# Attention and mixture of experts on one core: a planner's order against a written software pipeline of 25 iterations

## The chip, the core and the metric

The kernel runs on one core of a Trainium2 chip. A core has four engines that compute: TensorE (PE; its weight loads are listed apart as PEld), VectorE (DVE), ScalarE (ACT) and GpSimd (POOL). SyncE (SP) issues most of the transfers here; sixteen DMA engines carry them out. Each engine works through its own queue in order, and waits on semaphores for the others. The metric is the device time of one execution in microseconds (us).

## What is computed

An attention over 8 batches of 8 heads, with 576 positions of 64 elements, gives 4608 rows of 512; a mixture of 8 experts then works on these rows. Cut to what matters:

```python
def _attn_ref(q, k, v):
    q_d, k_d, v_d = mean over each 4 positions       # 144 pooled positions
    out_up = np.repeat(sm_attn(q_d, k_d, v_d), 4, axis=2)
    mask = np.abs(pos[:, None] - pos[None, :]) < 4   # a band of 7 positions
    scores = np.where(mask, scale * q @ k.T, -1e9)
    out_local = softmax(scores) @ v
    return out_up + out_local

def _moe_ref(x, ...):
    logits = x @ w_gate + modality_bias[modality_id]
    e_idx = np.argmax(logits, axis=1)
    for e in range(8):
        h = np.maximum(x[e_idx == e] @ w1[e], 0.0)
        out[e_idx == e] = gate_w[...] * (h @ w2[e])
```

All inputs and outputs are float32.

## The kernel before

The attention runs over 32 steps, one for each pair of heads (b, hp): 8 batches of 4 pairs. Step n of the loop in `build` (L764) holds pieces of several pairs at once.

- `load_qk` (L188) loads q and k of two pairs in eight transfers of [96 partitions, 6 rows of 64]; `load_v` (L199) loads a batch's v in 23 windows of up to 32 positions into `vw`, one buffer for even and one for odd batches; `load_vg` (L213) loads v of one pair for the pooling. All are issued from SP.
- `pre` (L225) transposes q and k on TensorE (L238) into PSUM tiles of tag T, which has three buffers, copies them out on ACT (q, L243) and DVE (k, L245), and adds up groups of four (DVE L248, POOL L252 and L253). `pool_v` (L217) does the same for v on POOL.
- `scores` (L259), one step later: the band scores as 46 small matmuls (L275) on a mask, whose maxima and differences DVE takes (L278, L279), the exponential (L280), and the pooled scores (L286) with their maximum (DVE L290) and exponentials (ACT L294).
- `softmax` (L297), two steps later: sums and reciprocals (DVE L301 to L304), products on POOL (L306, L317), a 32x32 transpose on DVE (L309) and four copies on ACT that lay the weights out as a band in the buffer `Pw` (L312). Three buffers `Pw` take turns.
- `av` (L316), three steps later (LAG): transposes of the pooled weights (PE L327, ACT L330), products with v (L334, evicted as `Od` by ACT at L337; L344), and their sum into the tile X (DVE L352). The second batch of a pair starts 64 columns into its tile, so that the last 64 positions of the first go into X of the next.
- The router works once a batch: `logits` (L386, L388), `choose` (16 small DVE instructions and an exponential, L399 to L422), `place` (PE L429 to L433, DVE L436 to L440), `scatter` (four or five indirect transfers from POOL into a table, L445) and `rows` (PE L459, ACT L460 and a transfer from SP, L462), which writes the rows back for the experts.

The order in which an engine's queue holds these pieces is set by a planner, which takes the program's order as priority, puts instructions where its own model of time says that they are ready, and adds the semaphores. Some pieces have a higher priority (`hip`). A constant table adds six matmuls on a zero tile at step 4 (BZ, L777). In the steps from 25 on, two first groups of rows are gathered for the experts ("early", L837 to L848), and their matmuls start while the attention still runs. After the attention come 18 groups of 256 rows and one of 128, each with the weights of one expert, split into a high and a low part.

Of the kernel before, what the change touches and what calls it, by code (L numbers as in the profile page):

```python
# [42 lines left out]
N0,N1,N2 = (2,3,4)  # L43
PV = 0
AN = 2
LEAD = 8
ST = 1
NPW = 3
# [4 lines left out]
HIP = 1  # L53
GO = 1
LS = 1
VD = 0
NCE = (2,1,1)
BZ = (0,0,0,0,6)
# [104 lines left out]
class Attention:  # L163
    def __init__(s, tc, ctx, ectx, C, psum, q, k, v):
        s.tc, s.C, s.ps = tc, C, psum
        nc = s.nc = tc.nc
        s.q, s.k, s.v = q, k, v

        s.ld = ectx.enter_context(tc.tile_pool(name="ald", bufs=2, side="right", reuse_waits="tile"))
        s.wk = ctx.enter_context(tc.tile_pool(name="awk", bufs=2, reuse_waits="tile"))  # L170
        s.one = ctx.enter_context(tc.tile_pool(name="aone", bufs=1, reuse_waits="tile"))
        s.QK, s.V, s.VG = {}, {}, {}
# [3 lines left out]
        s.clear(0)  # L176

    def clear(s, j):

        nc = s.nc  # L180
        if j < 2:
            nc.vector.memset(s.kT[j][:, 0:PAD], 0.0)
            nc.vector.memset(s.kT[j][:, S + PAD :], 0.0)
            nc.vector.memset(s.vw[j][0:32, 0], 0.0)
            nc.vector.memset(s.vw[j][64:96, NB - 1], 0.0)
        (nc.vector if j == 0 else nc.gpsimd).memset(s.Pw[j], 0.0)

    def load_qk(s, b, half):  # L188
        nc = s.nc

        qt = s.ld.tile([96, 2, 6, 2, D], F32, name="qt")
        kt = s.ld.tile([96, 2, 6, 2, D], F32, name="kt")
        for g in range(2):
            for t, src in ((qt, s.q), (kt, s.k)):
                for a in range(2):
                    nc.sync.dma_start(t[:, g, :, a], src[b, 4 * half + 2 * g + a].rearrange("(j p) d -> p j d", j=6))
        s.QK[b, half] = (qt, kt)

    def load_v(s, b):  # L199
        nc = s.nc  # L200
        vd = s.wk.tile([72, H, 2, D], F32, name="vd")
        vw = s.vw[b % 2]
        s.V[b] = (vw, vd)

        for i in range(NB):
            for j in range(4):
                lo = BLK * i + SUB * j - PAD
                k0, k1 = max(lo, 0), min(lo + WIN, S)
                if lo + PAD < S:
                    nc.sync.dma_start(vw[32 * j + k0 - lo : 32 * j + k1 - lo, i],  # L210
                                      s.v[b, :, k0:k1].rearrange("h p d -> p h d"))

    def load_vg(s, b, hp):  # L213
        vg = s.VG[b, hp] = s.ld.tile([72, 2, 512], F32, name="vg", bufs=2)
        s.nc.sync.dma_start(vg, s.v[b, 2 * hp : 2 * hp + 2].rearrange("h (p t) d -> p h (t d)", t=8))

    def pool_v(s, b, hp):  # L217
        nc = s.nc
        v5 = s.VG.pop((b, hp)).rearrange("p h (c t d) -> p (h c) t d", c=2, t=4)
        t1 = s.ld.tile([72, 4, 2, D], F32, name="vt", bufs=2)  # L220
        nc.gpsimd.tensor_tensor(t1, v5[:, :, 0:2], v5[:, :, 2:4], op=ALU.add)
        (nc.vector if VD else nc.gpsimd).tensor_tensor(
            s.V[b][1][:, 2 * hp : 2 * hp + 2].rearrange("p h c d -> p (h c) d"), t1[:, :, 0], t1[:, :, 1], op=ALU.add)

    def pre(s, b, hp):  # L225
        nc, C = s.nc, s.C
        outs = []
        for nm, src in zip("qk", s.QK[b, hp // 2]):
            if nm == "q":
                Tm = T = s.ld.tile([128, S], F32, name="qT")  # L230
            else:
                T = s.kT[hp % 2]
                Tm = T[:, PAD : PAD + S]
            for i in range(2):

                p = s.ps.tile([128, 3, 96], F32, name="tp", tag="T", bufs=3)
                for j in range(3):
                    nc.tensor.transpose(p[:, j, :], src[:, hp % 2, 3 * i + j].rearrange("p a d -> p (a d)"),  # L238
                                        C.ident[:96, :96])
                x = Tm[:, 288 * i : 288 * i + 288]  # L240
                p = p.rearrange("m j p -> m (j p)")
                if nm == "q":
                    nc.scalar.mul(x, p, QS)  # L243
                else:
                    nc.vector.tensor_copy(x, p)  # L245
            dd = s.wk.tile([128, 144], F32, name=nm + "d")
            if nm == "q":
                nc.vector.tensor_reduce(dd, Tm.rearrange("m (g t) -> m g t", t=4), op=ALU.add, axis=AX.X)  # L248
            else:
                d2 = s.ld.tile([128, 144, 2], F32, name="d2", bufs=1)  # L250
                T4 = Tm.rearrange("m (g t) -> m g t", t=4)
                nc.gpsimd.tensor_tensor(d2, T4[:, :, 0:2], T4[:, :, 2:4], op=ALU.add)  # L252
                nc.gpsimd.tensor_tensor(dd.rearrange("m (c g) -> m g c", c=2),  # L253
                                        d2[:, :, 0].rearrange("m (g c) -> m g c", c=2),
                                        d2[:, :, 1].rearrange("m (g c) -> m g c", c=2), op=ALU.add)
            outs += [T, dd]
        return outs

    def scores(s, b, hp, qT, qd, kT, kd):  # L259
        nc, C = s.nc, s.C  # L260
        n = 2 * NB
        m = s.wk.tile([128, n], F32, name="lm")
        e = s.wk.tile([128, n, WIN], F32, name="le", bufs=3)
        for a in range(2):
            p = s.ps.tile([128, NB, WIN], F32, name="sc", tag="S", bufs=3)
            r = slice(64 * a, 64 * a + 64)
            g = slice(NB * a, NB * a + NB)
            nc.tensor.matmul(p, C.identb, C.mask, start=True, stop=False, skip_group_check=True)
# [11 lines left out]
        nc.scalar.activation(e, e, AF.Exp, scale=0.125 / QS)  # L280
        el = e
        p = s.ps.tile([128, 3, 144], F32, name="scd", tag="S", bufs=3)
        for c in range(3):
            for a in range(2):
                r = slice(64 * a, 64 * a + 64)
                nc.tensor.matmul(p[r, c, :], qd[r, 40 * c : 40 * c + 64], kd[r, :], start=True, stop=True,  # L286
                                 skip_group_check=True)
        m = s.wk.tile([128, 3], F32, name="dm")
        e = s.wk.tile([128, 3, 144], F32, name="de", bufs=3)
        nc.vector.tensor_reduce(m, p, op=ALU.max, axis=AX.X, negate=True)  # L290

        z = s.wk.tile([128, 5, 4], F32, name="z")
        for c in range(3):
            nc.scalar.activation(e[:, c], p[:, c], AF.Exp, bias=m[:, c : c + 1], accum_out=z[:, 4, c : c + 1])  # L294
        return el, (e, z)

    def softmax(s, b, hp, e, de):  # L297
        nc = s.nc
        n = 2 * NB
        ed, z3 = de  # L300
        nc.vector.tensor_reduce(z3[:, :4, :3], e.rearrange("p (r c) w -> p r c w", c=3), op=ALU.add, axis=AX.X)  # L301
        z = s.wk.tile([128, n + 3], F32, name="zr")
        nc.vector.tensor_scalar(z, z3[:, :, :3], 1e-9, None, op0=ALU.add)
        nc.vector.reciprocal(z, z)  # L304
        Pw = s.Pw[(4 * b + hp) % NPW]
        nc.gpsimd.tensor_tensor(e, e, z[:, :n].unsqueeze(2).broadcast_to([128, n, WIN]), op=ALU.mult)  # L306

        eT = s.wk.tile([128, n, WIN], F32, name="lt")
        nc.vector.transpose(eT.rearrange("p n w -> p (n w)"), e.rearrange("p n w -> p (n w)"))  # L309
        for j in range(4):  # L310
            r = slice(32 * j, 32 * j + 32)
            nc.scalar.copy(Pw[r, :, j, :SUB], eT[r, :, :SUB])  # L312
        if 4 * b + hp < AN:
            for c in range(3):
                nc.scalar.mul(ed[:, c], ed[:, c], z[:, n + c : n + c + 1])
        else:  # L316
            nc.gpsimd.tensor_tensor(ed, ed, z[:, n:].unsqueeze(2).broadcast_to([128, 3, 144]), op=ALU.mult)  # L317
        return Pw, ed

    def av(s, b, hp, Pw, Ed, dst):  # L320
        nc, C = s.nc, s.C
        vw, vd = s.V[b]
        PdT = s.wk.tile([72, 2, 2, 144], F32, name="PdT")
        for kc in range(2):
# [5 lines left out]
            nc.scalar.copy(PdT[:, kc].rearrange("p a (c r) -> p c a r", c=3), src)  # L330
        pd = s.ps.tile([128, 144], F32, name="avd", tag="A", bufs=2)
# [4 lines left out]
        Od = s.wk.tile([128, 144], F32, name="Od")  # L336
        nc.scalar.mul(Od, pd, 0.25)  # L337
        for i0, i1 in ((0, 3), (3, NB)):
            t0, t1 = BLK * i0, min(BLK * i1, S)
# [6 lines left out]
            p = p.rearrange("m i j q -> m (i j q)")  # L346
            for x, r0, r1, off in dst:
# [4 lines left out]
                nc.vector.tensor_tensor(  # L352
# [384 lines left out]
def build(tc, q, k, v, mid, w_gate, bias, w1, w2, out):  # L737
    nc = tc.nc
    with ExitStack() as ctx:
# [8 lines left out]
        with ExitStack() as actx:  # L748
# [6 lines left out]
            at.load_qk(0, 0)  # L755
            at.load_qk(0, 1)
            C.load(tc, cp, work, ro.wk, mid, bias, w_gate)
            at.load_v(0)
            at.load_vg(0, 0)
            steps = [(b, hp) for b in range(B) for hp in range(4)]  # L760
            hip = (lambda: tc.high_priority()) if HIP else ExitStack
            N = len(steps)
            st, X = {}, {}
            for n in range(N + LAG):  # L764
                if n < N:
                    b, hp = steps[n]
                    if hp % 2 == 0 and n + 2 < N and n > 0 or n == 0:
                        b2, h2 = steps[n + 2]
                        if (b2, h2 // 2) not in at.QK:
                            at.load_qk(b2, h2 // 2)  # L770
                    if n % 4 == 3 and b + 1 < B:
                        at.load_v(b + 1)
                    st[n] = at.pre(b, hp)
                if n < NPW - 1:
                    at.clear(n + 1)
                if n < len(BZ):
                    C.busy(nc, BZ[n])  # L777
                if n == N0:
# [160 lines left out]
```

## Time and profile before

| | us |
|---|---|
| median of three runs | 808.2 |
| lowest and highest | 801.91, 811.26 |
| the profiled execution's time | 799.32 |
| its span, first to last instruction | 797.6 |

A profile was taken of one execution, with each instruction's start, duration and waits. In its lines, L12 is line 12 of the kernel; `out<-in` are tiles; a number behind x is a count. A line of a group ends with the engine's idle time ahead of these instructions and what ended it. A line of the queue of SP or of another engine's own transfers has a q (SPq, POOLq). Busy times over the span, as shares: PE 93%, DVE 59%, ACT 53%, POOL 40%. The transfers moved 150.00 MB in 205075 packets, of which 132683 are under 512 bytes: a row of 64 elements of q, k or v is 256 bytes.

### The profile page before, as it was taken

The page shows a single profiled execution, that of the slowest core. Times are in us where ns is not written, and L with a number is a line of the kernel's source. Part 1 is how long each engine was busy: PE and PEld are TensorE (multiplying, and loading weights), DVE is VectorE, ACT ScalarE, POOL GpSimd, SP SyncE. Part 2 cuts the span into 40 slices and gives each one's busy share as a digit, 9 for nine tenths or more (in the row PEclk, how much of TensorE's full clock was granted, in tenths as well). Part 3 has the DMA queues.
Part 4 walks back from the last instruction along what each step waited for, and adds up shares of the span by engine and source line. Part 5 has one row for each costly group of instructions (what it writes and reads, how often), then busy time and mean ns, then how long its engine had stood idle before and what let it go on. Part 6 is the DMA issues. An engine that isn't in the chain of part 4 may idle for free. (4 is left out here: it accounts for less than half of the span.)

```text
span 797.6 us, 20726 instructions
## 1 busy us (share of the span) xinstructions
PE 739.1 (93%) x8185; PEld 616.6 (77%) x8185; DVE 469.4 (59%) x957; ACT 426.5 (53%) x882; POOL 319.2 (40%) x362
## 2 busy tenths in 40 slices
PE   8488999899989988899799999999999999999995
PEld 5366767576767666778699888999998899999884
DVE  7534757574657667858476555556555555655520
ACT  4534657474747356855466555545555554555520
POOL 5525565665574658323353333233222333222000
PEclk9685989897989679999989999999999999999998
DMA  8769967577868597334889766677666667666500
GB/s 143 149 135 179 202 132 201 104 177 138 209 125 210 98 235 189 110 108 176 283 275 321 253 207 227 213 249 237 229 227 220 216 225 233 224 217 231 186 13 18
DMA packets 205075, 150.00 MB, mean 188 GB/s; under 512 B 132683, under 2 KB 171631, under 8 KB 204976
## 3 DMA queue, kind: packets, MB, share of 16 engines
q1 hardware_dynamic: 196720, 129.43, 59.5%
q0 software_dynamic: 8256, 19.22, 6.8%
q8 instruction: 65, 1.06, 0.6%
q14 instruction: 34, 0.28, 0.2%
HBM read 129.40 MB, written 19.47 MB: 187 GB/s over the span
## 5 line engine op out<-in xcount | busy, mean ns | idle before, releaser
L613 DVE TENSOR_TENSOR wlo<-raw,whi 128x1024 fp32r<-128x1024 f32 x130 | 160.2, 1245 | 130.4 <-ACT whi L612 120.7
L612 ACT CAST whi<-raw 128x1024 fp32r<-128x1024 f32 x130 | 134.7, 1049 | 120.2 <-PE l L677 54.3
L677 PE MATMUL l<-xh,whi 128*128 128x256 f32 x488 | 138.8, 286 | 0.7 <-ACT xh L660 0.7
L677 PE MATMUL l<-xh,wlo 128*128 128x256 f32 x488 | 138.4, 284 | 0.0
L677 PE MATMUL l<-xl,whi 128*128 128x256 f32 x488 | 138.3, 284 | 0.0
L728 POOL DMA_INDIRECT out_dram<-o,tg x37 | 40.9, 1105 | 173.3 <-ACT o L727 127.7
L724 PE MATMUL l<-wlo,hh 128*128 128x512 f32 x256 | 100.4, 393 | 0.0
L724 PE MATMUL l<-whi,hl 128*128 128x512 f32 x256 | 100.4, 393 | 0.0
L724 PE MATMUL l<-whi,hh 128*128 128x512 f32 x256 | 98.7, 397 | 0.0
L677 PEld LDWEIGHTS l<-xh,whi 128*128 128x128 f32 x488 | 93.3, 192 | 2.5 <-ACT xh L660 1.1
L677 PEld LDWEIGHTS l<-xl,whi 128*128 128x128 f32 x488 | 93.4, 191 | 0.6
L677 PEld LDWEIGHTS l<-xh,wlo 128*128 128x128 f32 x488 | 93.3, 191 | 0.2 <-issue 0.2
L275 PEld LDWEIGHTS sc<-kT,qT 64*26 64x26 f32 (+1 forms) x2944 | 40.7, 104 | 36.6 <-issue 27.3
L275 PE MATMUL sc<-kT,qT 64*26 64x32 f32 (+1 forms) x2944 | 60.7, 199 | 8.9 <-issue 8.4
L626 POOL DMA_INDIRECT tg<-tab,midx x33 | 38.1, 1154 | 75.3 <-DMA out_dram<-o,tg 69.5
L680 DVE SCALAR_TENSOR_TENSOR hl<-l,hh 128x512 fp32r<-128x512 f32 x72 | 49.3, 685 | 24.8 <-ACT hh L679 24.8
L312 ACT COPY Pw<-lt 32x312 f32<-32x312 f32 x128 | 57.7, 451 | 10.4 <-DVE lt L309 8.3
L636 POOL DMA_INDIRECT xg<-xs,tg x37 | 43.3, 1170 | 47.6 <-DMA tg<-tab,midx 29.7
L679 ACT ACTIVATE hh<-l 128x512 fp32r<-128x512 f32 x72 | 42.8, 594 | 32.4 <-PE l L677 29.2
L724 PEld LDWEIGHTS l<-whi,hl 128*128 128x128 f32 x256 | 48.1, 188 | 10.7 <-issue 0.5
L724 PEld LDWEIGHTS l<-wlo,hh 128*128 128x128 f32 x256 | 48.0, 188 | 10.8
L724 PEld LDWEIGHTS l<-whi,hh 128*128 128x128 f32 x256 | 48.1, 188 | 10.6 <-issue 0.5
(203 smaller groups left out, 1444.1 us busy)
## 6 DMA issues: line engine op xcount, KB each, us to landing
raw<-in_moe_w_dram SPq DMA_DIRECT2D x152, 512.0 KB
vw<-in_v_dram SPq DMA_DIRECT2D x168, 64.0 KB
qt<-in_q_dram SPq DMA_DIRECT2D x64, 144.0 KB
kt<-in_k_dram SPq DMA_DIRECT2D x64, 144.0 KB
vg<-in_v_dram SPq DMA_DIRECT2D x32, 288.0 KB
xs<-R SPq DMA_DIRECT2D x36, 256.0 KB
xg<-xs,tg POOLq DMA_INDIRECT x37
out_dram<-o,tg POOLq DMA_INDIRECT x37
```

Of the source, the lines that this page charges most:

```text
L275: nc.tensor.matmul(p[32 * j : 32 * j + q1 - q0, i, :], qT[r, q0:q1], kT[r, q0 : q0 + WIN], start=False, stop=(i == NB - 1), skip_group_che ...
L312: nc.scalar.copy(Pw[r, :, j, :SUB], eT[r, :, :SUB])
L612: nc.scalar.copy(hi, raw)
L613: nc.vector.tensor_tensor(lo, raw, hi.bitcast(F32), op=ALU.subtract)
L626: nc.gpsimd.indirect_dma_start(out=T[:, h, :], out_offset=None, in_=s.tab[:, :], in_offset=bass.IndirectOffsetOnAxis(ap=idx[:, u, h : h + ...
L636: s.gathered = nc.gpsimd.indirect_dma_start(out=R[:, h, :], out_offset=None, in_=s.xs[:n, :], in_offset=bass.IndirectOffsetOnAxis(ap=T[:, ...
L677: nc.tensor.matmul(p[:, f, :], a[:, k, fs], x[:, k, :], start=(k == 0 and i == 0), stop=(k == 3 and i == 2))
L679: nc.scalar.activation(hh[:, 2 * c : 2 * c + 2, :], p, AF.Relu)
L680: nc.vector.scalar_tensor_tensor(hl[:, 2 * c : 2 * c + 2, :], p, 0.0, hh[:, 2 * c : 2 * c + 2, :].bitcast(F32), op0=ALU.max, op1=ALU.subtract)
L724: nc.tensor.matmul(p, a[:, f, hs], x[:, f % 2, :], start=(f == 0 and i == 0), stop=(f == 7 and i == 2))
L728: nc.gpsimd.indirect_dma_start(out=s.out[:, :], out_offset=bass.IndirectOffsetOnAxis(ap=T[:, h, 0:1], axis=0), in_=o, in_offset=None, boun ...
```

## The change

Every function of the attention is cut into pieces, and a function `iteration(n)` names them in one fixed order. For n under MAN = 25 they are traced inside `tc.manual_schedule()`, so that each engine's queue holds them just in that order. From 25 on the same function is traced, and the planner orders it as before.

```diff
+NPW = 2
+NQK = 4
+PWG = 3
-BZ = (0,0,0,0,6)
+MAN = 25
...
+    def load_qk(s, n):
+        qt = s.ld.tile([96, 6, 2, D], F32, name="qt", bufs=NQK)
+        kt = s.ld.tile([96, 6, 2, D], F32, name="kt", bufs=NQK)
+        for t, src in ((qt, s.q), (kt, s.k)):
+            for a in range(2):
+                nc.sync.dma_start(t[:, :, a], src[b, 2 * hp + a].rearrange("(j p) d -> p j d", j=6))
...
+    def load_v(s, b, part, parts):
...
+                    for a, z in ((k0, k1),) if lo >= 0 else ((0, 28), (28, k1)):
+                        todo.append((i, 32 * j - lo, a, z))
+        for i, o, a, z in todo[part * len(todo) // parts : (part + 1) * len(todo) // parts]:
+            nc.sync.dma_start(vw[o + a : o + z, i], s.v[b, :, a:z].rearrange("h p d -> p h d"))
...
+    def spread(s, n, js):
+        for j in js:
+            r = slice(32 * j, 32 * j + 32)
+            (nc.gpsimd.tensor_copy if j >= PWG else nc.scalar.copy)(s.Pw[n % NPW][r, :, j, :SUB], s.lt[n][r, :, :SUB])
...
+            C.routing(tc, cp, work, ps)
+            ro.start(work)
+            C.biases(tc, cp, work, ro.wk, ps)
...
+            def load(n):
+                if n + 3 < N:
+                    at.load_qk(n + 3)
+                if n < N:
+                    at.load_vg(n)
+                if n < 2:
+                    at.load_v(0, n, 2)
+                elif n >= 3 and (n - 3) // 4 + 1 < B:
+                    at.load_v((n - 3) // 4 + 1, (n - 3) % 4, 4)
...
+            def routing(n):
+                b, i = divmod(n - 8, 4)
+                if 0 <= b < B - 1:
+                    if i == 0:
+                        ro.choose()
+                    ro.rows(i, i + 1 if i < 3 and n < N + LAG - 1 else ro.G)
+            def entry(n, i):
+                b, j = divmod(n - 8, 4)
+                t = 2 * (j - 2) + i
+                if j >= 2 and 0 <= b < EB and (i < 2 or j == 3) and t < ro.G:
+                    ro.scatter(ro.t0 + t, ro.t0 + t + 1)
+            def iteration(n):
+                if 2 <= n <= N + 1:
+                    at.sums(n - 2)
+                    at.norm(n - 2)
+                entry(n, 0)
+                load(n)
+                routing(n)
+                if LAG <= n:
+                    at.turn_pooled(n - LAG)
+                if n < N:
+                    for i in range(2):
+                        at.turn(n, "q", i)
+                        at.turn(n, "k", i)
+                if n > LAG:
+                    at.add(n - 1 - LAG, to(n - 1 - LAG))
+                if n % 4 == 1 and 9 <= n < N + 2:
+                    ro.place()
+                if n < N:
+                    at.pool_q(n)
+                    at.pool_k(n)
+                entry(n, 1)
+                if LAG <= n:
+                    at.spread(n - LAG, range(4))
+                entry(n, 2)
+                if 1 <= n <= N:
+                    at.local(n - 1)
+                    at.pooled(n - 1)
+                if n % 4 == 3 and 7 <= n:
+                    ro.logits(...)
+                if LAG <= n:
+                    at.av_pooled(n - LAG)
+                    at.av_local(n - LAG)
+                if 1 <= n <= N:
+                    at.local_exp(n - 1)
+                    at.pooled_exp(n - 1)
+                    at.pool_v(n - 1)
+                if 2 <= n <= N + 1:
+                    at.turn_local(n - 2)
...
+            with tc.manual_schedule():
+                for n in range(MAN):
+                    iteration(n)
+            for n in range(MAN, N + LAG):
+                iteration(n)
```

What moves, piece by piece:

- Loads: q and k of one pair an iteration, three ahead, instead of two pairs in every other step; v of the next batch in four parts of six, one an iteration (the first batch in two parts of twelve). The first window of a batch, 29 positions, is cut into 28 and 1, so that a batch has 24 transfers instead of 23.
- Router: one part of `rows` an iteration, the scatters singly at three places of two iterations, `choose` in the first and `place` in the second iteration of a batch. Its tables and the filling of its table in memory (`routing`, `start`, `biases`) stand ahead of the loop, where they were in steps 2 to 4.
- The sum into X (`add`) of a pair stands one iteration later, and the 64 late positions of an even batch go into a tile of their own, `late`, which POOL copies into the next X.
- Buffers: `Pw` two instead of three, the exponentials `le` and `de` two instead of three, q and k four of one pair instead of two of two pairs.
- One of the four copies into `Pw` is on POOL; the pooled products of the first two pairs, which ACT did in three pieces each, are on POOL as all others.
- The six matmuls on a zero tile at step 4 are gone.
- The early experts' steps stand at n = 25, 27, 28, 30, 31 and 32 instead of 25, 26, 27, 29, 30 and 32. What follows the loop for the last batch is the same work, now written behind the loop.

More of the change, by code (lines that the diff above doesn't have):

```diff
@@ L323, in av @@
-        PdT = s.wk.tile([72, 2, 2, 144], F32, name="PdT")
+        Ed = s.ed.pop(n)
+        PdT = s.PdT[n] = s.wk.tile([72, 2, 2, 144], F32, name="PdT")
         for kc in range(2):
```

322 lines of the change are left out of this document (138 added, 184 removed).

## The prediction

> **What bounds the kernel now.** I read the page first.
>
> ```profile
> span 797.6 us, 20726 instructions
> PE   8488999899989988899799999999999999999995
> DMA  8769967577868597334889766677666667666500
> ```
>
> From slice 20 on TensorE is full: that is the MoE part, which the change doesn't edit. In the attention before it no engine is full, and the transfers come in swells. To count iterations I use one instruction that occurs once in each, the eviction Od (L337). It is issued in the third iteration after its loads (n - LAG), so its first occurrence belongs to iteration 3. Rows of its line, up to 250 us and for the whole run, then the window between the first and the twenty-second mark:
>
> ```profile
> L337 ACT ACTIVATE Od<-avd x22: 271/290/315, 38.2 to 249.1; 128x144 f32<-128x144 f32 x22
> ...
> L337 ACT ACTIVATE Od<-avd x32: 271/290/315, 38.2 to 350.4; 128x144 f32<-128x144 f32 x32
> ...
> 37.70:249.00 211.30, 192.35 (x3461) 140.62 (x3459) 125.06 (x385) 117.62 (x360) 116.24 (x143) 0.86 0.75 160
> ```
>
> Iterations 4 to 24 take 249.1 - 38.2 = 210.9 us, 10.04 each; 25 to 34 take (350.4 - 249.1)/10 = 10.1 each. Columns of a window: length, busy time of PE, PEld, DVE, ACT and POOL with counts, clock, DMA share, GB/s. Per iteration this window has 125.06/21 = 5.96 us of DVE, 5.60 of ACT, 5.54 of POOL, 6.70 of weight loads and 165 matmuls. Nothing is busy for 10 us (PE's 9.2 counts its modelled latencies), so the loop is bound by waits. Stretches of 20 us show where:
>
> ```profile
> 80.00:100.00 20.00, 19.75 (x390) 14.88 (x386) 14.79 (x48) 12.76 (x40) 10.89 (x13) 0.98 0.90 202
> 100.00:120.00 20.00, 18.39 (x306) 13.04 (x304) 10.51 (x28) 10.82 (x35) 11.78 (x16) 0.83 0.68 131
> 120.00:140.00 20.00, 19.13 (x394) 14.24 (x392) 14.70 (x50) 13.66 (x41) 11.50 (x14) 1.00 0.78 205
> 140.00:160.00 20.00, 16.64 (x269) 12.14 (x265) 10.62 (x32) 10.12 (x29) 12.80 (x17) 0.83 0.55 97
> 160.00:180.00 20.00, 17.99 (x421) 13.74 (x417) 15.38 (x48) 14.55 (x48) 12.13 (x16) 1.00 0.79 185
> 180.00:200.00 20.00, 18.64 (x274) 13.41 (x275) 9.40 (x25) 8.29 (x27) 11.81 (x15) 0.75 0.70 132
> 200.00:220.00 20.00, 19.84 (x390) 14.65 (x390) 13.83 (x49) 13.84 (x42) 10.50 (x14) 1.00 0.85 214
> 220.00:240.00 20.00, 17.41 (x275) 12.16 (x274) 11.05 (x35) 9.00 (x27) 13.31 (x17) 0.83 0.66 122
> ```
>
> The rate swings with a period of one batch. At 165 matmuls an iteration, the four full stretches (mean x399) run at 8.3 us an iteration, the four thin stretches (mean x281) at 11.7. What stands in the thin stretches, from the waits between 37 and 249 us, the DMA queue and the trace in order of time:
>
> ```profile
> POOL vt L221 <- DMA vg<-in_v_dram: 31.0, 9, 10.9
> POOL le L306 <- DVE zr L304: 28.7, 9, 5.8
> ACT PdT L330 <- PE pdt L327: 27.0, 17, 6.9
> PEld sc L275 <- issue: 22.3, 63, 2.8
> ...
> SPq L210 <- PE avl L344: 14.7, 8, 7.6
> ...
> 150.81 4.49 SPq L210 DMA_DIRECT2D vw<-in_v_dram  x5
> 155.41 0.36 SPq L215 DMA_DIRECT2D vg<-in_v_dram  x1
> ...
> 142.86 0.97 POOL L445 DMA_INDIRECT tab<-ig,si  x1 [0.30 <-issue]
> ...
> 143.44 0.27 PE L275 MATMUL sc<-kT,qT 64*26 64x32 f32 x2 [1.16 <-issue]
> ```
>
> First, SP's queue holds a whole batch's 23 vw loads in a row, which themselves wait up to 7.6 us for the last reader of the buffer (avl), and the small vg load stands among and behind them. POOL runs in order and waits for vg at L221, up to 10.9 us, while the le product (L306) that feeds the next transpose stands behind it. Second, four or five scatters (L445) come back to back, and while they run PE issues its small sc matmuls with gaps, with no wait shown. Third, the clock falls after such a hole.
>
> **The change part by part.**
>
> *Loads.* Each iteration now issues four q/k loads (three iterations ahead), one vg and a quarter of the next batch's vw (six of 24). Rows of these lines, min/median/max ns:
>
> ```profile
> L196 SPq DMA_DIRECT2D qt<-in_q_dram x64: 312/654/2761, 0.8 to 288.8; - x64
> L210 SPq DMA_DIRECT2D vw<-in_v_dram x184: 232/448/4539, 12.8 to 282.3; - x184
> L215 SPq DMA_DIRECT2D vg<-in_v_dram x32: 306/422/3714, 27.9 to 309.8; - x32
> L462 SPq DMA_DIRECT2D xs<-R x36: 320/350/542, 87.6 to 371.1; - x36
> ```
>
> SP's issue time is 4 x 0.654 + 6 x 0.448 + 0.422 + 1.1 x 0.350 = 6.1 us an iteration, under any loop I forecast. The bytes are the same: 160 GB/s x 10.04 us = 1.61 MB an iteration, 194 GB/s at 8.3 us, which the stretches at 80 and 200 us carried (202 and 214). By share, 0.75 x 10.04 = 7.5 us of sixteen engines: that is the floor of the transfers, and cover enough at 8.3. vg keeps one iteration's lead, the last quarter of vw too. What the loads cost at a stall, the 31.0 us at L221 and most of the 28.7 at L306, goes; next in line is DVE's own chain.
>
> *Fixed order.* The loop is then what its slowest in-order chain takes, and DVE is the one I find, because ACT hands it tiles in order. Mean durations, ns after the second bar's comma:
>
> ```profile
> L294 ACT ACTIVATE de<-scd,dm 128x144 f32<-128x144 f32 x60 | 22.0, 378 | 2.3 <-DVE gt L420 1.4 <-DVE dm L290 0.8
> L330 ACT COPY PdT<-pdt 72x288 f32<-72x288 f32 x42 | 15.8, 393 | 32.8 <-PE pdt L327 27.0 <-remote 5.6
> L460 ACT COPY R<-xr 128x512 f32<-128x512 f32 x22 | 12.4, 588 | 5.1 <-PE xr L459 1.9 <-PE tp L238 1.7 <-DMA xs<-R 1.4
> L301 DVE TENSOR_REDUCE z<-le 128x12 f32<-128x384 f32 x20 | 10.9, 544 | 12.4 <-ACT le L280 12.2
> L309 DVE STREAM_TRANSPOSE lt<-le 128x384 f32<-128x384 f32 x19 | 10.8, 570 | 9.4 <-POOL le L306 9.3
> L304 DVE RECIPROCAL zr<-zr 128x15 f32<-128x15 f32 x20 | 4.9, 245 | 0.3
> ...
> 161.72 0.41 PE L238 MATMUL tp<-ident,kt 96*128 96x96 f32 x3
> ```
>
> Waits that the written order leaves on DVE: (a) the reciprocal (sums) needs three exps, 3 x 0.378 plus an accumulator read of about 0.2 = 1.33 us, while DVE has lt and z to do, 1.11: 0.22. (b) The first kT copy needs transposes whose PSUM buffer (three of tag T) is freed by R and then PdT on ACT: 0.588 + 0.393 + 0.41 = 1.39 after the exps, less about 0.4 for the reciprocal and its addition: 0.99. (c) The second needs PdT again, qT (about 0.4) and transposes: 0.36 beyond the first copy. Sum 5.96 + 1.57 = 7.53. The router's choose and place steps lie in the 5.96; the exp in choose (L418) stops ACT's queue, R and PdT behind it, once a batch. I take 8.3, the rate of the full stretches, which have all this work in them; the low end is 7.5 (this sum, and the transfers' floor), the high end 9.5 if choose, place and logits hold the in-order queues 4 to 5 us a batch more.
>
> *Moved to POOL.* One of four Pw copies leaves ACT, where it took 0.451. POOL has no such row; the nearest are these.
>
> ```profile
> L252 POOL TENSOR_TENSOR d<-kT 128x288 f32<-128x288 f32 x21 | 13.9, 664 | 15.4 <-DVE kT L245 14.2 <-PE scd L286 1.1
> L253 POOL TENSOR_TENSOR kd<-d 128x144 f32<-128x144 f32 x20 | 9.0, 450 | 0.9
> L317 POOL TENSOR_TENSOR de<-de,zr 128x432 f32<-128x432 f32 x19 | 17.2, 905 | 0.0
> ```
>
> 312 elements lie between 0.45 and 0.91; I take 0.66, nearest in size. POOL then has 5.54 + 0.66 = 6.2 of 8.3. The two or three scatters of an iteration (0.97 each plus 0.30 of issue) now stand between other pieces; in two iterations of four POOL reaches about 8.5, so DVE's transpose at the iteration's end is late next; inside the range. The late tile adds four POOL copies of 256 columns, about 0.6 each, hidden. PE's gaps beside scatters (22.3 us) remain in part, below PE's slack.
>
> *Removed.* Six filler matmuls at n = 4, a third Pw buffer, third le and de buffers. Each reuse is two iterations off and its last reader is done in the iteration before: nothing, unless an engine runs two iterations ahead, which the order forbids. [...]
>
> *Start.* Iteration 3's av needs the first vw, now behind 12 + 3 + 2 + 17 + 17 = 51 issues instead of 42, which took until 27.9 us:
>
> ```profile
> 27.90 0.74 SPq L215 DMA_DIRECT2D vg<-in_v_dram  x2
> 13.13 3.02 SPq L210 DMA_DIRECT2D vw<-in_v_dram  x1
> ```
>
> At (27.9 - 0.8)/42 = 0.645 each, the last is out at 33.7, and Od at about 36.5 with landing (38.2 before). The router's tables, now ahead of the loop, could cost up to 8 us if the order makes PE wait for them, but only the part past 33.7 would count. The 3.02 us issue follows the first vw load of 29 rows; the change cuts it into 28 and 1. [...]
>
> *Sum.* Iteration 24 at 36.5 + 21 x 8.3 = 210.8 instead of 249.1: 38.3 us less. Iterations 25 to 34 stay with the planner at about 10.1, early experts one iteration later, and the MoE is unchanged: 0. The profiled execution took 799.3 (span 797.6): 761. It lies 8.9 under the median of the three runs and 2.6 under the lowest; I add 6: 767.
>
> **The rivals.**
>
> *Faster still.* Loop 7.5: 36.5 + 157.5 = 194, 55 us less, 750. For it: the chain above; against: no 20 us stretch before reached it with the same transfers beside.
>
> *Given back.* The last ten iterations or the router's chain into the first experts lose half of it (the planner now starts from another state, or the loop runs at 9.2): 786. For it: nothing after iteration 24 is written by hand.
>
> *No change.* Loads and scatters only coincide with a limit of another kind, and the loop stays at 10.04: 803. Against: full and thin stretches hold the same code.
>
> *Slower: PE at half clock.* The written order puts a short PE wait for PSUM buffers into every iteration. Weight loads show the size: 13.74 us at clock 1.00 for x417 is 5.4 us an iteration, 10.8 at half clock, so a cold iteration is PE-bound at 10.8: 36.5 + 227 = 263, 14 us later, 819. It decides once some 70% of iterations are cold (8.3 + 2.5x = 10.04). For it:
>
> ```profile
> 60.00:80.00 20.00, 17.52 (x210) 12.33 (x210) 8.51 (x22) 8.84 (x25) 11.32 (x14) 0.51 0.95 179
> ```
>
> Against: the full stretches have such waits at 0.98 to 1.00. [...]
>
> **How the numbers follow.** Forecast (752 to 780) 0.50; faster still 0.15; given back (780 to 800) 0.18; no change 0.08; slower 0.09. About 1% (8 us) is what a measurement of this kernel can tell from no change. Faster 0.83, same 0.08, slower 0.09. The predicted time is the likeliest case's, 767; its own range is 752 to 780. 745 to 804 leaves out some 2 in 10: the far part of the faster case, and most of the last two.
>
> **What would show it.** Right: the Od marks 8 to 8.6 us apart up to iteration 24, without a batch's period; no wait of L221's successor for vg; clock near 1.0 after 40 us; DMA share above 0.85 in the loop. Wrong: clock near 0.5 in the loop; POOL's queue as the one that all wait for; an Od mark at 38 us that comes past 45; more than 10.5 us between later marks or a longer hole before the MoE becomes full.

## The result: slower by 3.9%, and the profile after

| | us | ratio to before |
|---|---|---|
| before, median of four runs | 806.9 (801.91 to 811.26) | 1 |
| after, median of four runs | 837.68 (835.82 to 840.09) | 1.0385, 95% interval 1.0317 to 1.0453 |

The prediction was 767.0, with a range of 745 to 804: the kernel became slower, not faster, and its time lies outside the range. From the first page of the changed kernel (busy tenths in forty slices, then the granted clock and the share of the DMA engines):

```profile
span 835.4 us, 20876 instructions
PE   6688687785968766899979999999999999999995
DMA  9898666674857387014578996666667676666600
```

Before, PE was full from the twenty-first slice on (0.9 or more); now it is full from the twenty-second, each slice 5% longer, and the transfers have a hole from the seventeenth to the nineteenth that was not there. The rows of Od, up to iteration 24 and for the whole run:

```profile
L361 ACT ACTIVATE Od<-avd x22: 290/290/291, 30.4 to 267.4; 128x144 f32<-128x144 f32 x22
...
L361 ACT ACTIVATE Od<-avd x32: 286/290/305, 30.4 to 390.6; 128x144 f32<-128x144 f32 x32
```

The windows between these marks (columns as in the prediction):

```profile
30.40:267.40 237.00, 181.45 (x3478) 148.15 (x3479) 137.50 (x391) 111.78 (x350) 132.72 (x175) 0.81 0.72 148
267.40:390.60 123.20, 100.66 (x1523) 77.17 (x1522) 72.74 (x201) 61.17 (x169) 67.90 (x82) 0.81 0.47 129
```

The 37.8 us of span come from two stretches. The start is 7.8 earlier (30.4, not 38.2). The written loop takes 237.0 rather than 210.9 (+26.1). The planner's last ten iterations take 123.2 rather than 101.3 (+21.9). What follows them is 2.4 shorter (835.4 - 390.6 against 797.6 - 350.4). PE's busy time in the loop fell by ten (181.45 against 191.95 in the same stretch before): PE is not slower, it is kept waiting. Sorted by n modulo 4, iterations 9 to 24 take 12.5, 9.5, 8.6 and 16.7 us for 0, 1, 2 and 3. The long ones follow the iterations 10, 14, 18 and 22, the first that scatter. The waits from 40 to 260 us say for what:

```profile
DVE kT L245 <- PE tp L240: 49.0, 28, 8.6
...
POOL Pw L336 <- DMA tab<-ig,si: 37.5, 8, 7.0
PEld avl L375 <- POOL Pw L336: 33.2, 9, 5.3
PE avl L375 <- POOL Pw L336: 30.4, 9, 5.1
...
ACT R L496 <- PE xr L495: 24.6, 8, 6.4
ACT ex L454 <- DVE L L440: 17.8, 4, 6.7
```

One of them in order of time, on POOL, PE, DVE and ACT (start, duration, instruction, idle time before it):

```profile
94.69 0.99 POOL L481 DMA_INDIRECT tab<-ig,si  x1
100.16 0.44 POOL L336 COPY Pw<-lt 32x312 f32<-32x312 f32 x1 [4.48 <-DMA tab<-ig,si]
...
100.65 2.26 PE L375 MATMUL avl<-Pw,vw 128*64 128x104 f32 x24 [5.04 <-POOL Pw L336]
102.84 1.12 PE L495 MATMUL xr<-ident,X 128*128 128x128 f32 x4
...
105.96 0.46 DVE L245 COPY kT<-tp 128x288 f32<-128x288 f32 x1 [7.84 <-PE tp L240]
...
104.00 0.58 ACT L496 COPY R<-xr 128x512 f32<-128x512 f32 x1 [6.36 <-PE xr L495]
```

The scatter occupies POOL for 0.99 us; the Pw copy behind it starts 5.5 us after the scatter did, when the scatter has landed in the table. The copy has nothing to do with the table. PE's avl waits for it, and since PE's order is fixed, xr, the turns and everything behind them wait too; then DVE and ACT. In the trace, up to 400 us, 23 instructions of POOL's queue wait on the semaphores that tell of the scatters' landing, and all 23 belong to this copy, on partitions 96 to 127; no other POOL instruction of the attention waits on them.

### The profile page after: what moved, and what is told of

Its sections match the earlier page's. It is cut to its first block, busy times and chain, and to the rows that moved or that the text cites. A ratio compares the mean times of both kernels' runs of the same rounds, so it can differ in the third digit from the quotient of the medians.

```text
span 835.4 us, 20876 instructions
## 1 busy us (share of the span) xinstructions
PE 732.2 (88%) x8179; PEld 628.3 (75%) x8179; DVE 480.2 (57%) x956; ACT 412.0 (49%) x844; POOL 342.3 (41%) x400
## 5 line engine op out<-in xcount | busy, mean ns | idle before, releaser
L375 PE MATMUL avl<-Pw,vw 128*64 128x104 f32 (+1 forms) x768 | 57.4, 309 | 34.7 <-POOL Pw L336 34.3
L375 PEld LDWEIGHTS avl<-Pw,vw 128*64 128x64 f32 (+1 forms) x768 | 50.6, 176 | 41.4 <-POOL Pw L336 37.4
L662 POOL DMA_INDIRECT tg<-tab,midx x33 | 42.4, 1286 | 73.7 <-DMA out_dram<-o,tg 66.0
L245 DVE COPY kT<-tp 128x288 f32<-128x288 f32 x64 | 28.9, 453 | 65.4 <-PE tp L240 63.3
L672 POOL DMA_INDIRECT xg<-xs,tg x37 | 43.0, 1163 | 48.1 <-DMA tg<-tab,midx 30.6
L760 PEld LDWEIGHTS l<-whi,hh 128*128 128x128 f32 x256 | 48.1, 188 | 10.5 <-issue 0.5
```

The lines of the kernel that those rows point to most:

```text
L375: nc.tensor.matmul(p[64 * a : 64 * a + 64, i - i0, :J, :], vw[: 32 * J, i, 2 * hp + a, :], Pw[: 32 * J, NB * a + i, :J, :SUB], start=True, ...
L662: nc.gpsimd.indirect_dma_start(out=T[:, h, :], out_offset=None, in_=s.tab[:, :], in_offset=bass.IndirectOffsetOnAxis(ap=idx[:, u, h : h + ...
L672: s.gathered = nc.gpsimd.indirect_dma_start(out=R[:, h, :], out_offset=None, in_=s.xs[:n, :], in_offset=bass.IndirectOffsetOnAxis(ap=T[:, ...
L760: nc.tensor.matmul(p, a[:, f, hs], x[:, f % 2, :], start=(f == 0 and i == 0), stop=(f == 7 and i == 2))
```

## The experiments

The theory (A) is that this wait alone made the kernel slower; its rivals stand in the expectations. All kernels below are the changed one with an edit, or the kernel before with one. Marks and lengths are from the Od rows of one profiled execution each, which need not be the median one: that of kernel 2 took 810.16 us, 8.5 over its median, and that of kernel 6 801.48, 6.7 over. The intervals are of the ratio to the kernel before, run beside each kernel. Its median was 812.3 beside 1 to 4, 807.5 beside 5, 6, 8 and 10, 805.9 beside 11 to 14 and 805.6 beside 7, 9 and 15, so kernels of different groups are compared by the ratio and not by the median.

| kernel | median us | ratio, 95% interval | n = 3 at | per iteration, 4 to 24 | 25 to 34, us |
|---|---|---|---|---|---|
| before | 806.9 | 1 | 38.2 | 10.04 | 101.3 |
| after | 837.7 | 1.032 to 1.045 | 30.4 | 11.29 | 123.2 |
| 1 POOL's copy at partition 0 | 808.8 | 0.991 to 0.998 | 31.3 | 9.63 | 123.6 |
| 2 all copies on ACT | 801.6 | 0.975 to 0.990 | 30.7 | 10.00 | 120.7 |
| 3 scatters behind the copy | 811.2 | 0.997 to 1.005 | 34.6 | 9.87 | 121.9 |
| 4 the planner throughout | 825.3 | 1.004 to 1.023 | 37.7 | 10.17 | 125.1 |
| 5 as 1, rows in two iterations | 801.9 | 0.991 to 0.999 | 31.8 | 9.59 | 117.9 |
| 6 as 1, old order from 25 | 794.8 | 0.981 to 0.994 | 32.2 | 9.75 | 116.0 |
| 7 as 6, three Pw buffers | 795.5 | 0.978 to 0.994 | 31.3 | 9.48 | 118.1 |
| 8 before, new loads alone | 804.0 | 0.993 to 1.002 | 36.4 | 10.47 | 94.5 |
| 9 before, spread rows alone | 808.0 | 0.996 to 1.005 | 39.3 | 9.67 | 119.1 |
| 10 as 1, written through 32 | 794.1 | 0.979 to 0.993 | 30.3 | 9.71 | 111.1 |
| 11 as 10, copy at 96 again | 846.2 | 1.045 to 1.056 | 31.3 | 11.03 | 131.1 |
| 12 as 10, ex moved | 781.9 | 0.964 to 0.974 | 32.2 | 9.30 | 107.9 |
| 13 as 10, rows moved | 793.0 | 0.974 to 0.991 | 31.7 | 9.25 | 116.1 |
| 14 as 10, both moved | 797.3 | 0.981 to 0.994 | 30.6 | 9.53 | 115.8 |
| 15 as 12, ex an iteration later | 787.0 | 0.970 to 0.983 | 30.9 | 9.20 | 111.4 |

**The wait of the copy (1, 2, 3, 4, 11).** Kernel 1 changes one comparison, so that POOL copies partitions 0 to 31 and ACT the others:

```diff
-(nc.gpsimd.tensor_copy if j >= PWG else nc.scalar.copy)(...)
+(nc.gpsimd.tensor_copy if j < 1 else nc.scalar.copy)(...)
```

> The one of the four Pw copies that POOL makes is that of partitions 0 to 31 rather than 96 to 127; the work is the same on every engine. Theory A (in the changed kernel that copy waits for the landing of the scatters that stand before it on POOL, 6 to 7 us each time, and PE, DVE and ACT wait behind it in their fixed order): no idle time before the Pw copy that a scatter ends, iterations 4 to 24 from 11.25 us to 8.5 to 9.2, mark 24 at 215 to 225 us, the time 780 to 800. Rival B (the fixed order itself, or PE at half clock, makes the long iterations): the iterations stay at 11 to 11.5 us and the time at 830 to 845. Rival C (POOL has too much to do with the copy): as B, POOL just ends its idle time otherwise.

The idle time before this line that a scatter ends, 40.7 us over the whole run, is gone; the waits that are left at it are for DVE, its transpose `lt` above all. The copy no longer waits for a scatter's semaphore anywhere in kernel 1's trace, and the longest time that POOL's queue spends on a semaphore ahead of it falls from 5.906 us to 0.017. The rows of the line, first after, then kernel 1:

```profile
L336 POOL COPY Pw<-lt x32: 442/443/450, 33.8 to 381.4; 32x312 f32<-32x312 f32 x32
L336 POOLq EVENT_SEMAPHORE  x29: 17/43/5906, 100.0 to 381.1; - x29
...
  DMA tab<-ig,si: 40.7, 9
```

```profile
L336 POOL COPY Pw<-lt x32: 437/438/486, 32.8 to 347.4; 32x312 f32<-32x312 f32 x32
L336 POOLq EVENT_SEMAPHORE  x10: 17/17/17, 239.0 to 347.3; - x10
...
  DVE lt L329: 8.6, 7
```

The loop fell from 237.0 to 202.2 us (233.5 - 31.3). Rivals B and C fall, as each expected no effect. The forecast of 780 to 800 was missed: the last ten iterations stayed at 123.6, so their loss is not the wait's, and the loop stopped at 9.63, above the 8.5 to 9.2 expected.

Kernel 2 takes the copy off POOL:

```diff
-PWG = 3
+PWG = 4
...
                 at.spread(n - LAG, range(4))
-                entry(n, 2)
...
                     at.turn_local(n - 2)
+                entry(n, 2)
```

> All four Pw copies on ACT, and the third scatter of an iteration moved to the iteration's end. Theory A: as with the copy on partitions 0 to 31, plus 0.6 us an iteration on ACT, which has slack: 780 to 805, iterations 8.5 to 9.5 us. Rival B: 830 to 845. Rival C: 780 to 805 while the copy on partitions 0 to 31 stays near 835. If the scatters delay POOL's other work (norm, d, kd) by their own time, the iterations with scatters stay longer than the others by 2 us or more here too.

The time came out within its range, at 801.6; the iterations did not: 10.00 us, above the 8.5 to 9.5 expected, though in an execution 8.5 us slower than the median. Kernel 3 keeps the copy at partition 96 and moves each scatter behind it, so that those before it are older:

```diff
-                entry(n, 0)
+                entry(n - 1, 2)
...
-                entry(n, 1)
                 at.spread(n - LAG, range(4))
-                entry(n, 2)
+                entry(n, 0)
...
+                entry(n, 1)
```

> POOL keeps the copy on partitions 96 to 127; the scatters are moved to behind it and to the iteration's end, so the scatters that stand before a copy are most of an iteration old. Theory A: the wait is still there but mostly met: 790 to 815, idle time before the Pw copy ended by scatters from 40 us to under 12. Rival B: 830 to 845. Rival C: 825 to 845.

The time fits theory A, the wait does not: it was halved, not cut to a third. Its row at L336:

```profile
  DMA tab<-ig,si: 21.3, 7
```

Kernel 4 sets `MAN = 0`:

> The planner orders all 35 iterations; the new pieces, loads and the POOL copy on partitions 96 to 127 stay. Theory A: the copy waits for scatters here as well, whatever their place, so the time lies between 810 and 850 and the POOL rows show that wait. Rival B (the written order costs the time): 790 to 812, that is, at the kernel before or faster.

825.3 lies in theory A's range and above rival B's. The copy waits for scatters under the planner too, 9.5 us and 6.4 more for a gather. The loop is that of before (10.17 against 10.04 us an iteration), and the loss lies in the last ten iterations (125.1). The planner with POOL's copy on partitions 0 to 31 was not run, so how much of this loss is the wait's stays open. That the written order is not what makes the kernel slow is shown by kernel 1, which keeps the order and loses the wait. Kernel 11 puts the copy back to partitions 96 to 127 (`j >= PWG`) in kernel 10, described below:

> As the kernel with the written order through iteration 32, but POOL's Pw copy is again that of partitions 96 to 127. Theory A: the wait for scatters comes back, iterations 4 to 24 at 11 us or more, the time 818 to 835. If the wait mattered only through the planner's last iterations: 794 to 802.

```profile
  DMA tab<-ig,si: 64.2, 12
  DMA xg<-xs,tg: 2.6, 1
```

It came out 52 us over kernel 10 (846.23 against 794.08), more than expected. Of the 47.9 us between the two profiled spans, 27.6 lie in the loop and 20.0 in the last ten iterations, where the scatters come close together. So the wait was taken out (1) and put back (11), and the time followed it both times.

**The last ten iterations (5 to 10).** Kernel 5 makes the rows 2 and 3 at a time again from iteration 28 on:

```diff
-                    ro.rows(i, i + 1 if i < 3 and n < N + LAG - 1 else ro.G)
+                    if n < 28:
+                        ro.rows(i, i + 1 if i < 3 and n < N + LAG - 1 else ro.G)
+                    elif i < 2:
+                        ro.rows(2 * i, (2, ro.G)[i])
```

> As the kernel with POOL's copy on partitions 0 to 31 (n = 24 to 34 takes 124 us there, 101 before the change), and from iteration 28 on the router's rows are made in two iterations, 2 and 3 at a time, as before the change, instead of one an iteration. Theory R (the row stores stand later in SP's queue and hold the weight loads and what waits for them): n = 24 to 34 in 100 to 112 us, the time 785 to 798. Rival O (it is the order in which the planner gets the attention's pieces) and rival L (the equal loads): 118 us or more, the time 802 to 815.

Kernel 6 traces iterations 25 on in the order of before, with three buffers of de; kernel 7 adds a third Pw (`NPW = 3`):

```diff
             for n in range(MAN, N + LAG):
-                iteration(n)
+                tail(n)   # turn(n), sums to spread(n - 2), local and pooled(n - 1),
+                          # values and add(n - 3), logits / choose, rows / place, rows
```

> As the kernel with POOL's copy on partitions 0 to 31, and from iteration 25 on the pieces are given to the planner in the order of the kernel before (turns, softmax, scores, then the values with their sum in the same iteration, then the router two iterations after its logits); the loads stay equal. Theory O: n = 24 to 34 in 98 to 110 us, the time 782 to 798. Rival L: 118 us or more, the time 802 to 815. Theory R gives the same as O here, as the rows go in twos and threes too.

> As the kernel whose pieces from iteration 25 on come in the order of before (n = 24 to 34 in 116 us), but with three buffers of Pw as before the change instead of two. If the missing buffer holds the planner's last ten iterations: n = 24 to 34 in 101 to 108 us, the time 784 to 792. If not: 113 to 119 us, 792 to 802.

Kernel 8 is the kernel before with the change's loads, kernel 9 the kernel before with a batch's rows over four iterations:

```diff
-                    if n % 4 == 3 and b + 1 < B:
-                        at.load_v(b + 1)
+                    if n + 3 < N:
+                        at.load_qk(n + 3)
+                    if n >= 3 and (n - 3) // 4 + 1 < B:
+                        at.load_v((n - 3) // 4 + 1, (n - 3) % 4, 4)
```

```diff
-                            ro.rows(0, 2)
+                            ro.rows(0, 1)
...
-                            ro.rows(2, 5)
+                            ro.rows(1, 2)
...
+                            ro.rows(2, 3)
...
+                        ro.rows(3, 5)
```

> The kernel before with the change's loads alone: queries and keys for one iteration at a time, three ahead, the values in quarters, 28 and 1 rows in place of 29. Theory A with R or O: the stalls of vt on its load go, the planner keeps its order: 795 to 810, iterations 4 to 24 in 9.7 to 10.1 us, n = 24 to 34 near 101 us. Rival L (the equal loads lengthen the last ten iterations): n = 24 to 34 in 115 us or more, the time 815 to 830.

> The kernel before with the change's rows alone: one an iteration over four iterations, in place of two and three over two. Theory R in the other direction: n = 24 to 34 from 101 to 108 to 118 us, the time 811 to 824. If the rows matter only together with the other pieces' order: within 1% of before, 799 to 813.

The equal loads are cleared: kernel 8 has the shortest last ten iterations of all. They are not a gain either, alone: its loop takes 10.47 us an iteration, above the 9.7 to 10.1 expected, and under the planner vt's wait for vg stays. From 40 to 250 us in kernel 8, then in the changed kernel from 40 to 268:

```profile
POOL vt L224 <- DMA vg<-in_v_dram: 44.3, 11, 7.4
```

```profile
POOL vt L224 <- DMA vg<-in_v_dram: 5.1, 1, 5.1
```

Kernel 4, which differs from the changed kernel in the planner alone, still waits 41.4 us there from 40 to 250 us. So that wait went with the written order of SP's queue. Spreading the rows alone (9) lengthens the last ten iterations by 17.8 us on the kernel before, as theory R said; its loop is 7.8 us shorter (203.1 against 210.9), and the time is the same within half a percent. One way it can: SP's queue takes stores and weight loads in turn, and a store waits for R. In the changed kernel five stores hold the queue for 46 us, and the weights stand behind them, which is the hole in the transfers:

```profile
324.92 46.15 SPq L498 DMA_DIRECT2D xs<-R  x5
373.79 0.39 SPq L633 DMA_DIRECT2D raw<-in_moe_w_dram  x1
```

But undoing the spreading (5), the order (6), or the order and the missing buffers (7) takes only 6 to 8 us off 123.6, no more than single executions differ by (those of before lie between 801.91 and 811.26). Theories R and O both predicted 112 or less and both fell short; kernel 7 came out in the range for the case that the buffer does not matter. For theory R this settles less than it seems, since kernel 5 did not free SP's queue. Its waits for R at these stores during the last ten iterations, in the kernel before and in kernels 1, 5 and 8:

```profile
SPq L462 <- ACT R L460: 13.2, 1, 13.2
SPq L498 <- ACT R L496: 32.8, 4, 15.1
SPq L498 <- ACT R L496: 37.9, 3, 34.7
SPq L465 <- ACT R L463: 2.2, 4, 0.8
```

The shortest wait and the shortest last ten iterations are both kernel 8's. But kernel 9 has 19.0 us of it and takes 119.1, and no run takes the wait away from the changed kernel: it is a candidate, not a shown cause.

Kernel 10 goes on with the written order through iteration 32, the early experts' steps and the later scatters included; a weight's split stands one iteration behind its load:

```diff
-            for n in range(MAN, N + LAG):
-                iteration(n)
+            with tc.manual_schedule():
+                for n in range(33):
+                    (iteration if n < MAN else late_iteration)(n)
+            for n in range(33, N + LAG):
+                late_iteration(n)
```

> As the kernel with POOL's copy on partitions 0 to 31, and the written order goes on through iteration 32, the early experts' steps included (counts in iteration 25, entries 28, rows 29, each weight split one iteration behind its load). If the planner's order makes the last ten iterations long (theories R and O alike): n = 24 to 32 at 9.5 to 10.5 us each, n = 24 to 34 in 100 to 108 us, the time 780 to 798. If the work added there (early experts, row stores, scatters) makes them long whoever orders them: 115 us or more, the time 800 to 815.

111.1: nearer to the planner's fault than to the work's, though not at the 100 to 108 asked for. The time, 794.1, is 1.4% under the kernel before.

**The loop without the wait (12 to 15).** At 9.71 us an iteration the loop of kernel 10 is still 1.4 over the forecast. Among its waits from 64 to 228 us:

```profile
DVE kT L245 <- PE tp L240: 23.6, 28, 2.6
...
ACT ex L454 <- DVE L L440: 13.0, 5, 3.4
PE tp L240 <- ACT R L496: 9.5, 7, 1.7
DVE zr L316 <- ACT de L309: 8.4, 17, 0.5
```

Kernel 12 cuts `choose` in two; the exponential and the three small DVE instructions behind it (`weigh`) stand behind the Pw copies. Kernel 13 moves the call of `rows` there, 14 both, 15 puts `weigh` at the start of the next iteration. Kernel 12:

```diff
-                        ro.choose()
+                        ro.choose(False)
...
                 entry(n, 2)
+                if n % 4 == 0 and 8 <= n < 4 * B + 4:
+                    ro.weigh()
```

> As the kernel with the written order through iteration 32, and the router's ex (with the three small operations behind it on DVE) moved from the routing at the iteration's start to behind the Pw copies, so that ACT does not stop for DVE's chain to L. Theory D (the fixed order stops an engine for the router's pieces): that wait (13.0 us in 5 iterations) goes, the iterations that hold choose from 11.0 to 9.5 us or less, 5 to 8 us in all, the time 785 to 790. Rival E (PE's own work and its half clock set the iteration): 792 to 797.

> As the kernel with the written order through iteration 32, and the router's rows (xr on PE, R on ACT, the store) moved from the iteration's start to behind the Pw copies. Theory D: the waits of PE's tp for R (17.8 and 12.2 us in 40 to 240 us) go, iterations 9 to 24 from 9.55 to 8.4 to 9 us, the time 772 to 785. Rival E: the wait moves to another tile, 790 to 797.

> Both moves at once. Theory D: iterations 9 to 24 at 8.0 to 8.8 us, the time 766 to 782. Rival E: 788 to 797.

> As the kernel with the written order through iteration 32 and ex moved, but ex and the three small DVE operations behind it stand at the start of the next iteration, ahead of DVE's wait for PE's tp, not ahead of the local maxima. If the 12.7 us of the iterations after choose come from these operations on DVE (theory D, its second form): those iterations fall to 10 to 11 us, 6 to 10 us in all, the time 770 to 777. If DVE's chain to L alone makes them long: 779 to 785.

Kernel 12 did better than theory D asked, and has the lowest ratio of all: 781.88 (781.09 to 782.86), 0.9691 of before (0.9640 to 0.9743). The iterations with choose fell from 11.0 to 8.1 us, but the next ones rose from 8.8 to 12.7, since `weigh` now stood ahead of DVE's maxima and ACT's exponential waited for them (among the waits of kernel 12 in the same window):

```profile
ACT le L287 <- DVE le L284: 11.4, 6, 2.9
PE tp L240 <- ACT R L503: 10.3, 6, 2.6
```

Kernel 15 removed that (12.7 to 9.9 us), as expected, and yet gained nothing in time: the iterations after it went from 7.4 to 8.8, the last ten from 107.9 to 111.4, and 787.0 lies above both its ranges. Kernels 13 and 14 missed theory D's times; 793.0 lies in rival E's range and 797.3 at its end. In kernel 13 the rows' wait for R turned into one of PE's tp for PdT (9.8 us, 12 times, from 64 to 228 us), as rival E had said of it. The gains do not add: the loop of kernel 12 is 8.7 us shorter than kernel 10's, that of 13 is 9.7 shorter, and with both moves (14) it is 3.9 shorter. All four loops lie between 9.2 and 9.5 us an iteration, far from 8.3.

## Why the prediction was wrong

Three terms failed. The first made the kernel slower; with it put right (kernel 1) the time is that of before, still far from the forecast. Kernel 1's span, 803.2, is 43.9 us over the 759.3 that the forecast's 761 stands for: 5.2 less at the start, 27.9 more in the loop, 22.3 more in the last ten iterations, 1.0 less behind them.

- **Moved to POOL** is the step that turned the sign. It priced the copy by its duration and found POOL at 6.2 of 8.3 us: "inside the range". The duration was even overestimated (0.66; measured 0.443). What it left out is that the copy got a wait: for the landing of the scatters ahead of it, 5.5 us after their start, where the step had counted the 0.97 us of their issue. It also did not ask who waits for the copy: avl on PE, and behind avl the whole fixed order. The wait is 34.8 us of the loop (237.0 less 202.2 in kernel 1).
- **Fixed order**, 8.3 us an iteration, named waits that are there, and its sum was too small. Without the copy's wait the loop takes 9.2 to 9.75 (kernels 1, 5 to 7, 10, 12 to 15; 10.00 in kernel 2), about the high end of 9.5 that the prediction gave for router pieces holding the in-order queues, and ex, R and choose's chain do hold them. 9.63 against 8.3 is 27.9 us over 21 iterations. DVE's window and its longest waits there, in kernel 1 from 31.3 to 233.5 us, show which terms were too small:

```profile
31.30:233.50 202.20, 171.46 (x3477) 139.07 (x3478) 141.85 (x394) 113.79 (x350) 130.94 (x173) 0.87 0.84 166
...
DVE kT L245 <- PE tp L240: 29.6, 32, 3.8
DVE z L314 <- ACT le L287: 10.7, 9, 3.3
DVE zr L316 <- ACT de L309: 9.1, 19, 0.5
```

  Per iteration, the wait for transposes (b and c) is 1.41 us, where the prediction had 1.35, and that for the exponentials (a) 0.43, where it had 0.22. The wait of z for le, 0.51, was not in the sum. DVE is busy for 6.75 us and not 5.96. The large instructions did not grow (the kT copy takes 0.45 us before and after); small ones of the router did, as the last section shows. In the changed kernel instructions also overlap less with their neighbours: from 30.4 to 267.4 us the durations of DVE's instructions add up to 151.4 us in 137.5 busy, where they came to 145.4 in 124.6 in the kernel before (38.2 to 249.1 us); for kernel 1 it is not shown.
- **Sum**, with the last ten iterations at "0", was off by 21.9 us. The rival "given back" named this place and priced it at 19 (786 less 767), close to what it cost. The spread rows lengthen it alone; why it stays 7 to 22 us longer than before in every version with a faster loop is not settled.
- **Start** was better than forecast (30.4, not 36.5), from a wrong dependence: Od needs the pooled values and PdT, not vw. Its first mark, at 30.4, comes before the second half of the first vw has all been issued.

```profile
24.31 8.39 SPq L212 DMA_DIRECT2D vw<-in_v_dram  x12
```

- **Loads** held: the 31.0 us at vt became 5.1, and the bytes are the same. The longest issue of a vw load went from 4.539 us to 1.547, though one in kernel 1 takes 3.340.

```profile
L212 SPq DMA_DIRECT2D vw<-in_v_dram x192: 311/448/1547, 14.3 to 311.4; - x192
```

The issue behind the first vw load takes 3.02 us in the kernel before and 3.21 in kernel 9, where that load has 29 rows; it takes 0.78 in the changed kernel and in kernels 1, 4, 8 and 10, where it has 28 and the issue behind it is that of the one row left. So the delay went where the load was cut; no run shows the reason.
- **Removed** held as far as it was tried: a third buffer Pw (7 against 6) changes nothing beyond the spread of the runs. No run puts the filler matmuls back, so what leaving them out did is not shown.
- **PE at half clock**, the slower rival, is not what happened. The clock in the loop was 0.81, under the 0.86 of before, but in the same order without the copy's wait it is 0.87 (kernel 1, in the window above), and 0.89 in kernel 12: it fell with the holes, it did not make them. That waits as short as the ones this rival counted on lower the clock is shown by no run.

```profile
32.20:227.50 195.30, 161.77 (x3476) 131.13 (x3476) 142.62 (x384) 114.58 (x350) 131.02 (x175) 0.89 0.88 171
```

- The signs named beforehand told the truth: the marks kept a batch's period and lay 11.29 us apart, over the 10.5 named, POOL's queue was the one that all wait for, and DMA's share in the loop was 0.72, not above 0.85.

## What to carry to other kernels

An instruction that moves to another engine can take over that engine's waits, as the copy did (up to 5.906 us): before pricing it by duration, list what stands ahead of it in its new queue, transfers in flight included, and who waits for it. In a written order such a wait reaches every engine, as it did here (behind the copy shown, 5.04 us on PE, 7.84 on DVE and 6.36 on ACT), so it is worth asking which form of the instruction (here, its first partition) carries no wait. And a gain in one stage is counted only with the stage behind it: here (kernel 1 against before) the loop won 8.7 us, and ten iterations that were left to the planner took back 22.3.

## What the runs showed of the hardware beyond expectation

A copy of 32 partitions by POOL took 0.44 us whether it began at partition 0 or 96, but the one that began at 96 had waits for the scatters ahead of it, up to 5.906 us at the semaphore, and the one at 0 had none. The wait is one that the built program carries; other first partitions were not run. The copy reads what DVE wrote, not what a scatter did; no run here shows why the one at 96 carries the wait and the one at 0 does not.

Small DVE instructions stretched while POOL worked without a pause. In kernel 1 one of 128x8 elements took 3.38 us, ending with POOL's de product, where most small ones behind it took 0.15 to 0.17:

```profile
253.34 3.38 DVE L525 TENSOR_TENSOR eexcl<-eincl,en 128x8 f32<-128x8 f32 x1
257.96 0.15 DVE L528 SCALAR_TENSOR_TENSOR eoff<-eexcl,ecap 128x8 f32<-128x8 f32 x1
...
253.27 0.67 POOL L257 TENSOR_TENSOR d<-kT 128x288 f32<-128x288 f32 x1
255.76 0.90 POOL L323 TENSOR_TENSOR de<-de,zr 128x432 f32<-128x432 f32 x1
```

It is not a single case. The router's cast `si`, in the kernel before and in kernel 10:

```profile
L440 DVE CAST si<-sf x8: 133/166/400, 96.4 to 369.7; 128x4 int32<-128x4 f32 x4, 128x5 int32<-128x5 f32 x4
L476 DVE CAST si<-sf x8: 158/1315/1329, 87.7 to 368.5; 128x4 int32<-128x4 f32 x4, 128x5 int32<-128x5 f32 x4
```

At 87.67 us in kernel 10 it starts 0.05 us ahead of POOL's vt product and ends within 0.03 us of it, 1.33 us later. Up to the last Od mark, the traces of before, after, kernel 1 and kernel 10 have 12, 9, 15 and 19 DVE instructions that took over 0.5 us and over 2.2 times the shortest of their shape. POOL computed during 98 to 99% of their time, and during 45 to 50% of the whole stretch. That is a coincidence in time seen in four traces, not a tested cause.
